# Attention followed by a squared-ReLU FFN in fp32: seven buffers for the unscaled output, loads issued ahead of stores, staged pieces of w_in

## The chip, the cores and the metric

The kernel runs on one core of a Trainium2 chip. The metric is the device time of one execution in microseconds (us). Engines are named as the profile names them: PE (TensorE, with PEld for its weight loads), DVE (VectorE), ACT (ScalarE), POOL (GpSimd) and SP (SyncE, which here only issues DMAs; SPq and ACTq are the queues of DMA issues).

## The reference

Eight batches, twelve heads, 448 tokens, 64 numbers a head. The attention's data are fp32, the two matrices of the FFN 64-bit floats; the result is fp32.

```python
q_n, k_n = rmsnorm(q, g_q), rmsnorm(k, g_k)
scores = q_n @ k_n.T / sqrt(64)
attn = exp(scores - max(scores)); attn /= sum(attn) + 1e-9
x = (attn @ v)               # as 3584 tokens x 768
h = x @ w_in                 # w_in 768 x 2048
g = s * relu(h) ** 2 + b
out = g @ w_out              # w_out 2048 x 768
```

## The kernel before

**Order of work.** The order of every engine's instructions is written out by hand: the program's order is the order on each engine and on each DMA queue. Almost all DMAs are issued by SP, one after the other; an issue that has to wait for its data or its buffer holds back all that SP issues later. Only the rows of q and k for the norms are loaded from ACT's queue (L189).

**Attention.** Two heads make a pair; there are 48 pairs, and each takes four slots of a software pipeline. `slot(i)` (L390) issues the scores, the exponentials and then the jobs that were put down for this slot (L373 to L388). For pair p these are: the load of `kqv` (L212; six buffers, so that of pair p-6 has to be free) in slot 4p-21, the spreading of the inverse norms (L219) in 4p-20, `weigh` (L294, L301: the product with v, and the sums of the exponentials on PE, in one PSUM tile `av`) in slots 4p+3 and 4p+5, and right after it `take`: ACT copies the sums to `sz` (L312, one buffer) and the unscaled output to `uz` (L313, four buffers). Later slots write the sums to DRAM and read them back across partitions (`gather` 4p+7, `fetch` 4p+9 into `zt`), invert them (DVE L324, slot 4p+12), write them and read them back spread (`put_z` 4p+13, `get_z` 4p+16), multiply on POOL (`divide` L340, 4p+18) and store x (`put_x` L343, 4p+20). Between these, 24 pieces of w_in are converted, one every seven slots (`convert` L345): the 64-bit numbers are read as two 32-bit words each and made into fp32 by DVE and ACT, and sums for the product are made by POOL. The pieces for the first four of eight column groups stay in SBUF split in two parts; the other twelve go to DRAM (`t_d`).

**The FFN's first product.** The product of 2x2 blocks is made by seven products of sums of blocks (`MUL`, L459), each in three matmuls of split operands (high x high, high x low, low x high). There are 14 runs (7 groups of 512 tokens, twice: first the column groups 0 to 3, then 4 to 7) of four blocks; n counts the 56 blocks, i the four of a run. One block, `ffn_in` (L463), is 63 matmuls of 256 columns into four PSUM banks. With eight banks, block n+1 takes those of block n-1, which `rectify` (L503) frees: ACT copies and DVE adds the seven products (L477 to L499), ACT applies the relu (L519) and SP stores r to DRAM (L520). After `ffn_in` of block n come, in this order: `rectify` of block n-1 with its store, late slots of the attention, the end of a conversion of w_out begun a block before, the begin of the next (its load, L561), and `steps(n)` (L692). `steps` prepares x for the next run, in three parts: `s_load` (SP, L441; two buffers), `s_sums` (POOL, L138 to L140), `s_split` (ACT L150, DVE L152; four buffers). In block i=0 it loads two parts, in i=1 it sums and splits the first, in i=2 it loads the third and sums the second, in i=3 it sums the third and splits the second and third. Conversions of w_out begin from n=4 on in all blocks but i=0, and from n=28 on in all. When the second half of the columns begins (n=25 to 28), `steps` also loads the twelve pieces of w_in from DRAM and splits them (`tin_load` L528, `tin_split`), through two buffers `w9`.

**The FFN's second product** (`g_load` to `store`, L579 to L657) is not touched by the change. At its end it uses the buffers `uz` of the long-lived pool for its split operand.

Of the kernel before, what the change touches and what calls it, by code (L numbers as in the profile page):

```python
# [45 lines left out]
def attention_then_relu2_ffn(  # L46
# [117 lines left out]
    def attention(ps):  # L164
# [142 lines left out]

        def take(p):
            t = avs.pop(p)
            uz = uzs[p] = lp.tile([P, 2 * TG], F32, tag="uz", bufs=4, name=f"uz{p}")  # L310
            sz = szs[p] = lp.tile([P, SEQ], F32, tag="sz", name=f"sz{p}")
            S.copy(sz, t[:, 1, :SEQ])  # L312
            S.copy(uz[:, :SEQ], t[:, 0, :SEQ])  # L313
# [133 lines left out]
    def s_sums(n):  # L447
        sums_right(s9s[n], G)

    def s_split(n):  # L450
        t = s9s.pop(n)
        to = sns[n] = pools["s"].tile([P, 2, 7, 2 * P], F32R, tag="s", bufs=NK + 1, name=f"s{n}")
        return split((to[:, 0], to[:, 1]), t[:, 1:8])

    def finish(g):
        for _ in g:
            pass
# [63 lines left out]
            r_d[q][g].rearrange("f p t -> p f t"), rt.rearrange("p (f t) -> p f t", f=2)  # L521
        )

    tls = {}

    def tin_load(q, k):
        t = tls[q, k] = pools["w9"].tile([P, 7, P], F32, tag="w9", bufs=2, name=f"tl{q}_{k}")
        nc.sync.dma_start(t.rearrange("p c f -> p (c f)"), t_d[q][k])  # L528

    def tin_split(q, k):  # L530
        to, of = t_in(q), tls.pop((q, k))
        return split((to[:, k, 0], to[:, k, 1]), of)

    touts = {}

# [128 lines left out]
    with tc.manual_schedule(engines=ORDERED):  # L664
# [4 lines left out]
        for i in range(FIRST, NSLOT + 2):  # L669
            slot(i)  # L670
            if i == NSLOT - 8:
                first.close()
                pools["s"] = pools["s9", 0] = pools["s9", 1] = pool(mid, "spool", "right")
            for n in range(NK):
                if i == NSLOT - 8 + 3 * n:
                    s_load(n)
                if i == NSLOT - 6 + 3 * n:
                    s_sums(n)
                if i == NSLOT - 5 + 3 * n:
                    finish(s_split(n))  # L680
        early.close()
        pools["w9"] = pools["t4"] = pool(ctx, "w9pool", "left")
        pools["c"] = pools["s9", 1] = pool(late, "cpool2", "left")
        ps = ctx.enter_context(
            tc.tile_pool(name="ps", bufs=1, space=PSUM, reuse_waits="tile")
        )
# [5 lines left out]
        def steps(n):  # L692

            r, g, q = blocks[n]
            i = q % QUADS
            s0 = NK * (r + 1)
            if r + 1 < len(runs):
                if i == 0:
                    s_load(s0)
                    s_load(s0 + 1)  # L700
                elif i == 1:
                    s_sums(s0)
                    finish(s_split(s0))
                elif i == 2:
                    s_load(s0 + 2)
                    s_sums(s0 + 1)
                else:
                    s_sums(s0 + 2)
                    finish(s_split(s0 + 1))
                    finish(s_split(s0 + 2))  # L710
            b = n - (NG - 1) * QUADS
            if b == 0:
                for k in range(2):
                    tin_load(QUADS, k)
            if 0 < b <= QUADS:
                u = b + QUADS - 1
                for k in range(NK):
                    finish(tin_split(u, k))
                    if k == 0:
                        tin_load(u, 2)  # L720
                    elif u + 1 < NM:
                        tin_load(u + 1, k - 1)
            if n == nb - 14:
                tout_load(0)
                tout_load(1)
            if n == nb - 13:
                finish(tout_split(0))
                finish(tout_split(1))
            b = n - (nb - QUADS)
            if b == 0:  # L730
                tout_load(2)
                tout_load(3)
            elif b > 0:
                for k in (2 * b, 2 * b + 1):
                    finish(tout_split(k))
                    tout_load(k + 2)

        for n, (r, g, q) in enumerate(blocks):
            ffn_in(r, q)
            if n:  # L740
                rectify(*blocks[n - 1])
            for i in range(3 * n, 3 * n + 3):
                if i < 20:
                    slot(NSLOT + 2 + i)
            for x in begun:
                finish(x)
            begun.clear()
            if n >= 4 and todo and (n % 4 or n >= 28):
                c = convert_out(todo.pop(0))
                next(c)  # L750
                begun.append(c)
            steps(n)
            if n == nb - QUADS - 1:
                assert not todo and not begun
                late.close()
                pools["g"] = pool(ctx, "gpool", "left")
                for x in range(3):
                    g_load(x)
            if n == nb - 3:
                g_sums(0)  # L760
                g_sums(1)
            if n == nb - 2:
                g_load(3)
                g_load(4)
# [70 lines left out]
```

## Time and profile before

| | us |
|---|---|
| median of 3 runs | 1820.38 |
| lowest and highest | 1816.62, 1824.65 |
| the profiled execution | 1828.55 |
| its span | 1826.7 |
| PE busy | 1465.4 (80%) |
| DVE, ACT, POOL busy | 1002.7, 775.2, 800.3 |

The profile is of one execution; its rows are read against that execution's own time. Busy times are sums over the span. A wait is put down to the event that came last before an instruction began. The three stages follow one another: attention to about 777 us, the first product to about 1389, the second to the end.

### The profile page before, as it was taken

What the parts mean: (1) busy time and instruction counts of PE and PEld (TensorE: products, weight loads), DVE (VectorE), ACT (ScalarE), POOL (GpSimd) and SP (SyncE); (2) the same over time, 40 slices, a digit from 0 to 9 for tenths busy, and PEclk for the clock granted to TensorE, in tenths of its full rate; (3) what the DMA queues carried; (4) which work ended last, traced back from release to release, by engine and by line L of the source; (5) the groups of instructions that cost most, each with busy time, mean ns of one, the idle gap of its engine ahead of it and who ended that gap; (6) DMA issues with size and microseconds to landing.
All of it is one profiled execution on the core that took longest, in us unless ns stands there. A gap on an engine that the chain in (4) does not pass through costs nothing. (4 is left out here: it accounts for less than half of the span.)

```text
span 1826.7 us, 26159 instructions
## 1 busy us (share of the span) xinstructions
PE 1465.4 (80%) x9760; PEld 1126.6 (62%) x9760; DVE 1002.7 (55%) x1546; ACT 775.2 (42%) x1132; POOL 800.3 (44%) x719
## 2 busy tenths in 40 slices
PE   2877777677777778898878756777887999999999
PEld 1433323233322333397877755777886899999999
DVE  3555544454444444345555555555456977767675
ACT  2555444453444444533333433333445544444443
POOL 6355544464444453333343322333321645555553
PEclk6998888898878988998989878888998999999999
DMA  7475545554656555334444444444336433333232
GB/s 212 123 192 155 152 131 147 163 164 140 170 151 183 156 157 160 88 106 156 133 139 140 146 148 150 143 135 135 135 112 217 151 94 104 100 94 104 93 109 65
DMA packets 172366, 253.71 MB, mean 139 GB/s; under 512 B 54544, under 2 KB 122832, under 8 KB 172240
## 3 DMA queue, kind: packets, MB, share of 16 engines
q1 hardware_dynamic: 165904, 231.86, 42.1%
q10 hardware_dynamic: 6336, 20.19, 3.5%
q8 instruction: 76, 1.25, 0.3%
q14 instruction: 50, 0.41, 0.1%
HBM read 183.06 MB, written 68.76 MB: 138 GB/s over the span
## 5 line engine op out<-in xcount | busy, mean ns | idle before, releaser
L471 PE MATMUL h<-s,tin 128*128 128x256 f32 x3528 | 485.2, 302 | 132.5 <-DVE r L480 57.4
L471 PEld LDWEIGHTS h<-s,tin 128*128 128x128 f32 x3528 | 469.5, 208 | 148.8 <-DVE r L480 63.9
L630 PE MATMUL m<-tout,gh 128*128 128x384 f32 x1568 | 404.1, 339 | 10.1 <-ACT gh L614 9.9
L294 PE MATMUL av<-e,kqv 128*32 128x448 f32 x1536 | 209.8, 674 | 163.8 <-ACT uz L313 162.2
L253 DVE TENSOR_REDUCE nmx<-sh 112x2 fp32r<-112x896 f32 x192 | 208.6, 1088 | 187.3 <-PE sh L244 180.9
L630 PEld LDWEIGHTS m<-tout,gh 128*128 128x128 f32 x1568 | 286.6, 190 | 11.8 <-ACT gh L614 10.8
L630 PE MATMUL m<-tout,gl 128*128 128x384 f32 x784 | 266.2, 339 | 5.9 <-DVE gl L615 5.9
L284 ACT ACTIVATE e<-st 128x896 f32<-128x896 f32 x192 | 176.4, 919 | 160.6 <-PE st L277 160.3
L294 PEld LDWEIGHTS av<-e,kqv 128*32 128x32 f32 x1536 | 45.3, 124 | 254.0 <-ACT uz L313 173.8
L594 POOL TENSOR_TENSOR g<-g 128x256 f32<-128x256 f32 x112 | 94.5, 844 | 226.6 <-DVE g L593 226.6
L273 PE MATMUL st<-kqv 64*128 64x448 f32 x768 | 182.1, 550 | 0.0
L152 DVE TENSOR_TENSOR s<-s,s 128x1792 fp32r<-128x1792 f32 x42 | 87.5, 2088 | 168.8 <-ACT s L150 165.7
L614 ACT CAST gh<-g 128x896 fp32r<-128x896 f32 x112 | 105.3, 941 | 174.0 <-POOL g L598 102.0
L615 DVE TENSOR_TENSOR gl<-g,gh 128x896 fp32r<-128x896 f32 x112 | 141.2, 1261 | 57.2 <-ACT gh L614 57.2
L480 DVE TENSOR_TENSOR r<-r,h 128x256 f32<-128x256 f32 x408 | 144.2, 415 | 39.9 <-ACT r L490 26.0
L230 POOL TENSOR_TENSOR kqv<-kqv,rb 128x448 f32<-128x448 f32 x95 | 129.8, 1376 | 66.9 <-ACT kqv L226 65.9
L340 POOL TENSOR_TENSOR uz<-uz 128x448 f32<-128x448 f32 x48 | 55.6, 1158 | 232.2 <-DMA uz<-z_d 217.3
L630 PEld LDWEIGHTS m<-tout,gl 128*128 128x128 f32 x784 | 148.4, 189 | 8.0 <-DVE gl L615 8.0
L277 PE MATMUL st<-shq,row 64*128 64x448 f32 x384 | 139.9, 720 | 3.8 <-DMA shq<-nmx 3.8
L244 PEld LDWEIGHTS sh<-kr 64*112 64x112 f32 x384 | 54.6, 278 | 140.6 <-issue 49.9
L200 DVE TENSOR_REDUCE ssq<-raw 128x14 f32<-128x896 f32 x48 | 52.1, 1085 | 159.3 <-ACT raw L195 108.5
L138 POOL TENSOR_TENSOR s<-s 128x512 f32<-128x512 f32 x42 | 55.1, 1311 | 186.3 <-DMA s<-x_d 172.1
(78 smaller groups left out, 1795.6 us busy)
## 6 DMA issues: line engine op xcount, KB each, us to landing
kqv<-in_dram SPq DMA_DIRECT2D x48, 704.0 KB
raw<-r_d SPq DMA_DIRECT2D x112, 256.0 KB
r_d<-r SPq DMA_DIRECT2D x51, 512.0 KB
rb<-i_d SPq DMA_DIRECT2D x96, 224.0 KB
raw<-in_dram ACTq DMA_DIRECT2D x44, 448.0 KB
w64i<-in_dram SPq DMA_DIRECT2D x24, 512.0 KB
w64o<-in_dram SPq DMA_DIRECT2D x32, 384.0 KB
uz<-z_d SPq DMA_DIRECT2D x96, 112.0 KB
```

Source lines behind the costliest of these rows:

```text
L230: E.tensor_tensor(of, of, rb[:, n], ALU.mult)
L253: V.tensor_reduce(out=nmxs[p][:, :, c : c + 1], in_=shs.pop(i)[:QC, :, :SEQ], op=ALU.max, axis=AX.X, negate=True,)
L273: T.matmul(st[:, j, :SEQ], t[d, 0, k0 : k0 + P], t[d, 1], start=True, stop=False)
L277: T.matmul(st[:, j, :SEQ], row[d], shq[p % 3][d], start=False, stop=True)
L284: S.activation(e, sts.pop(i)[:, :, :SEQ], AF.Exp)
L294: T.matmul(t[n * Q : (n + 1) * Q, 0, :SEQ], x[:, 2 * g + h, j, m * Q : (m + 1) * Q], e[h][:, j], start=g + h == 0, stop=g + h == 2,)
L471: T.matmul(to, w[:, lw, sa], x[:, lx, tb], start=k == n == 0 and j % 2 == 0, stop=k == NK - 1 and n == 2, skip_group_check=True,)
L480: V.tensor_tensor(to, to, part(j), op_)
L594: G.tensor_tensor(g9[:, 2:4], g9[:, 0:2], g9[:, 7:8].broadcast_to([P, 2, P]), ALU.add)
L614: S.copy(gh, g9[:, 1:8])
L615: V.tensor_tensor(gl, g9[:, 1:8], gh.bitcast(F32), ALU.subtract)
L630: T.matmul(to, g[:, sa], w, start=m == 0 and n == 0, stop=m == NM - 1 and n == 2,)
```

## The change

`take` takes three of seven `uz` tiles from the attention's own pool with three buffers, the other four as before from the long-lived pool. The four buffers of split x get a tag each, and the fourth is laid in a pool that opens when the attention's memory is given back. The loop over the blocks issues `s_load` and the begin of a conversion of w_out (its load) ahead of `rectify` with its store; conversions now begin from n=4 on in all blocks but i=2; the end of one is still worked in the block after its begin. `steps` sums two parts of x in block i=1 and the third in i=2. The pieces of w_in from DRAM go through one staging tile of six pieces: two are loaded in each of n=22, 23 and 24, and after each split the piece six further on.

```diff
         def take(p):
             t = avs.pop(p)
-            uz = uzs[p] = lp.tile([P, 2 * TG], F32, tag="uz", bufs=4, name=f"uz{p}")
+            if p % 7 < 2 or p % 7 == 6:
+                uz = ap.tile([P, 2 * SEQ], F32, tag="uz", bufs=3, name=f"uz{p}")
+            else:
+                uz = lp.tile([P, 2 * TG], F32, tag="uz", bufs=4, name=f"uz{p}")
+            uzs[p] = uz
...
     def s_split(n):
         t = s9s.pop(n)
-        to = sns[n] = pools["s"].tile([P, 2, 7, 2 * P], F32R, tag="s", bufs=NK + 1, name=f"s{n}")
+        n4 = n % (NK + 1)
+        to = sns[n] = pools["s", n4 < NK].tile([P, 2, 7, 2 * P], F32R, tag=f"s{n4}", name=f"s{n}")
...
-    def tin_load(q, k):
-        t = tls[q, k] = pools["w9"].tile([P, 7, P], F32, tag="w9", bufs=2, name=f"tl{q}_{k}")
-        nc.sync.dma_start(t.rearrange("p c f -> p (c f)"), t_d[q][k])
...
+    def tin_load(n):
+        if n >= QUADS * NK:
+            return
+        if not staged:
+            staged.append(pools["t4"].tile([P, 6, 7, P], F32, tag="t0", name="staged"))
+        q, k = divmod(n, NK)
+        nc.sync.dma_start(
+            staged[0][:, n % 6].rearrange("p c f -> p (c f)"), t_d[QUADS + q][k]
+        )
+
+    def tin_split(n):
+        q, k = divmod(n, NK)
+        to = t_in(QUADS + q)
+        return split((to[:, k, 0], to[:, k, 1]), staged[0][:, n % 6])
...
             if r + 1 < len(runs):
-                if i == 0:
-                    s_load(s0)
-                    s_load(s0 + 1)
-                elif i == 1:
+                if i == 1:
                     s_sums(s0)
+                    s_sums(s0 + 1)
                     finish(s_split(s0))
                 elif i == 2:
-                    s_load(s0 + 2)
-                    s_sums(s0 + 1)
-                else:
                     s_sums(s0 + 2)
+                elif i == 3:
                     finish(s_split(s0 + 1))
                     finish(s_split(s0 + 2))
             b = n - (NG - 1) * QUADS
-            if b == 0:
+            if -2 <= b <= 0:
                 for k in range(2):
-                    tin_load(QUADS, k)
+                    tin_load(2 * (b + 2) + k)
             if 0 < b <= QUADS:
-                u = b + QUADS - 1
                 for k in range(NK):
-                    finish(tin_split(u, k))
-                    if k == 0:
-                        tin_load(u, 2)
-                    elif u + 1 < NM:
-                        tin_load(u + 1, k - 1)
+                    finish(tin_split(NK * (b - 1) + k))
+                    tin_load(NK * (b + 1) + k)
...
         for n, (r, g, q) in enumerate(blocks):
             ffn_in(r, q)
-            if n:
-                rectify(*blocks[n - 1])
-            for i in range(3 * n, 3 * n + 3):
-                if i < 20:
-                    slot(NSLOT + 2 + i)
-            for x in begun:
-                finish(x)
-            begun.clear()
-            if n >= 4 and todo and (n % 4 or n >= 28):
+            i = q % QUADS
+            if r + 1 < len(runs):
+                if i == 0:
+                    s_load(NK * (r + 1))
+                    s_load(NK * (r + 1) + 1)
+                elif i == 2:
+                    s_load(NK * (r + 1) + 2)
+            begun_, begun[:] = begun[:], []
+            if n >= 4 and todo and i != 2:
                 c = convert_out(todo.pop(0))
                 next(c)
                 begun.append(c)
+            if n:
+                rectify(*blocks[n - 1])
+            for u in range(3 * n, 3 * n + 3):
+                if u < 20:
+                    slot(NSLOT + 2 + u)
+            for x in begun_:
+                finish(x)
             steps(n)
```

## Rows read from the trace of the kernel before

**Rows 1.** Windows by stage: length, then each engine's busy us; clock, DMA share.
```profile
102.95:716.11 613.16, 449.73 (x3054) 188.83 (x3050) 288.76 (x366) 272.66 (x375) 298.97 (x256) 0.86 0.57 158
...
776.85:1389.00 612.15, 485.02 (x3528) 469.47 (x3528) 328.40 (x629) 225.57 (x365) 206.74 (x174) 0.87 0.42 139
```

**Rows 2.** Attention, 102.95 to 716.11: a wait (us, times, longest); a group of instructions.
```profile
PE av L294 <- ACT uz L313: 159.1, 37, 6.6
...
L313 ACT COPY uz<-av 128x448 f32<-128x448 f32 x38 | 20.2, 533 | 206.0 <-DMA x_d<-uz 126.5 <-DMA rb<-i_d 49.5 <-issue 30.0
```

**Rows 3.** Timeline of a stalled pair: start, length, instruction, idle time before it.
```profile
416.00 0.35 SPq L212 DMA_DIRECT2D kqv<-in_dram  x1
...
416.46 0.56 SPq L343 DMA_DIRECT2D x_d<-uz  x1
...
423.97 0.53 ACT L313 COPY uz<-av 128x448 f32<-128x448 f32 x1 [6.32 <-DMA x_d<-uz]
...
424.56 3.22 PE L294 MATMUL av<-e,kqv 128*32 128x448 f32 x16 [5.26 <-ACT uz L313]
```

**Rows 4.** Pairs before the first stall: timeline of PE, and a window.
```profile
91.45 0.94 PE L301 MATMUL av<-e,ones 128*32 128x448 f32 x8
...
101.47 0.94 PE L301 MATMUL av<-e,ones 128*32 128x448 f32 x8
...
113.71 0.57 PE L244 MATMUL sh<-kr 64*112 64x448 f32 x2 [1.29 <-DVE nmx L253]
...
92.70:102.70 10.00, 10.00 (x82) 4.62 (x82) 7.73 (x11) 7.02 (x11) 5.35 (x4) 1.00 0.69 167
```

**Rows 5.** First product, 776.85 to 1389: waits (us, times, longest), PE's and SP's.
```profile
PE h L471 <- DVE r L480: 57.4, 15, 13.1
PE h L471 <- ACT s L150: 37.1, 16, 6.4
PE h L471 <- DVE s L152: 32.3, 21, 2.3
...
SPq L520 <- ACT r L519: 342.1, 38, 17.9
```

**Rows 6.** Timeline of PE: the first blocks of the first product.
```profile
776.85 37.01 PE L471 MATMUL h<-s,tin 128*128 128x256 f32 x294 [5.40 <-ACT uz L313]
```

**Rows 7.** Timeline of a run's first block: x load, sums, split, PE's bank.
```profile
996.78 2.57 SPq L441 DMA_DIRECT2D s<-x_d  x4
...
1004.10 1.29 POOL L138 TENSOR_TENSOR s<-s 128x512 f32<-128x512 f32 x1 [7.73 <-DMA s<-x_d]
...
1007.32 1.69 ACT L150 CAST s<-s 128x1792 fp32r<-128x1792 f32 x1 [8.97 <-POOL s L140]
...
1011.46 12.66 PE L471 MATMUL h<-s,tin 128*128 128x256 f32 x84 [6.01 <-DVE r L480]
```

**Rows 8.** Timeline of the last pair before the first stall: DVE, ACT, SP.
```profile
112.20 0.17 DVE L324 SCALAR_TENSOR_TENSOR zt<-zt 128x7 f32<-128x7 f32 x1 [3.17 <-DMA zt<-s_d]
...
114.95 0.53 ACT L312 COPY sz<-av 128x448 f32<-128x448 f32 x1 [2.01 <-DMA s_d<-sz]
...
101.71 0.33 SPq L212 DMA_DIRECT2D kqv<-in_dram  x1
...
112.96 0.39 SPq L212 DMA_DIRECT2D kqv<-in_dram  x1
```

**Rows 9.** Window of 2 us after a load of kqv; last the clock, DMA share, GB/s.
```profile
403.00:405.00 2.00, 1.27 (x10) 0.60 (x6) 1.58 (x3) 0.00 (x0) 2.00 (x3) 1.00 0.95 351
```

**Rows 10.** Timeline of DVE in a run's fourth block.
```profile
976.12 0.36 DVE L110 TENSOR_SCALAR o<-w64o 128x384 int32<-128x384 int32 x1 [4.52 <-DMA w64o<-in_dram]
```

**Rows 11.** The blocks that load pieces of w_in: a window, and timeline rows.
```profile
1042.00:1138.00 96.00, 63.38 (x443) 60.56 (x442) 51.70 (x89) 34.64 (x53) 26.55 (x24) 0.80 0.47 159
...
1075.34 0.94 ACT L150 CAST tin<-tl 128x896 fp32r<-128x896 f32 x1 [11.16 <-DMA tl<-t_d]
...
1078.61 5.16 PE L471 MATMUL h<-s,tin 128*128 128x256 f32 x21 [11.66 <-DVE r L480]
```

More of the change, by code (lines that the diff above doesn't have):

```diff
@@ L522, in rectify @@
         )
-    tls = {}
-    def tin_load(q, k):
-        t = tls[q, k] = pools["w9"].tile([P, 7, P], F32, tag="w9", bufs=2, name=f"tl{q}_{k}")
-        nc.sync.dma_start(t.rearrange("p c f -> p (c f)"), t_d[q][k])
-    def tin_split(q, k):
-        to, of = t_in(q), tls.pop((q, k))
-        return split((to[:, k, 0], to[:, k, 1]), of)
+    tls, staged = {}, []
+    def tin_load(n):
[11 more added lines that the diff above has]
+        return split((to[:, k, 0], to[:, k, 1]), staged[0][:, n % 6])
     touts = {}
@@ L672, in attention_then_relu2_ffn @@
                 first.close()
-                pools["s"] = pools["s9", 0] = pools["s9", 1] = pool(mid, "spool", "right")
+                pools["s", True] = pools["s9", 0] = pools["s9", 1] = pool(mid, "spool", "right")
             for n in range(NK):
@@ L683, in attention_then_relu2_ffn @@
         pools["c"] = pools["s9", 1] = pool(late, "cpool2", "left")
+        pools["s", False] = pool(mid, "spool2", "right")
         ps = ctx.enter_context(
```

## The prediction

> **What bounds the kernel now.** I read the windows by stage first, then the waits of TensorE (PE) in each stage, then the timelines of one stalled and one unstalled cycle. Of the span of 1826.7 us, 613 belong to 38 attention pairs and 612 to the first matrix product of the FFN [rows 1]; PE is busy 450 of the first and 485 of the second. So two stages have room; the last product, busy nearly throughout, has none.
>
> In the attention one wait explains nearly all idle time of PE: 159.1 us, 37 times, on the copy of `uz` (L313), and ScalarE itself sits idle 206.0 us ahead of 38 such copies [rows 2]. The timeline tells why [rows 3]. SP stands at the load of `kqv` until PE has used an older one; at 416.00 it goes, and only then the store of x of four pairs back (L343, 416.46). That store frees the buffer which the copy needs; the copy starts at 423.97, and PE, which waits for the bank that it empties, at 424.56 after 5.26 us of idling. So PE releases SP, SP's transfer releases ScalarE, and that PE: a ring that closes once a pair. 613.16/38 = 16.1 us a pair.
>
> What a pair costs without the ring is seen before the four buffers were used up: the last matmul groups of two pairs stand at 91.45 and 101.47, 10.02 us apart, with PE busy 10.00 of 10 us at a granted clock of 1.00 [rows 4]. In the stalled stage the mean clock is 0.86 [rows 1], so the stall also costs clock.
>
> In the FFN's first product PE waits 57.4 us for rectify's sums (banks not free), 37.1 for ScalarE's half of the split of x and 32.3 for VectorE's half [rows 5]. An undisturbed stretch gives 37.01 us for 294 matmuls, 0.126 us each [rows 6]; 3528 of them [rows 1] would be 444 us. The stage is 168 us above that: 127 of idling and 41 of slower matmuls. SP spends 342.1 us before the stores of r, waiting for the relu [rows 5], and everything queued behind waits too. In one such case the x load is issued at 996.78, lands at 1004.10, the sums on POOL are followed by the split at 1007.32, and rectify, behind that split on VectorE, frees PE's bank at 1011.46, after 6.01 us [rows 7].
>
> **The change, part by part.** *Seven buffers of uz.* The three p%7 classes in the attention's pool and the four in the long-lived one each rotate so that pair p reuses p-7's buffer. Its store is issued at slot 4p-8 and the copy stands at 4p+5, over three pairs later; before it was one slot. The wait goes; no instruction is added. The 206 us of ScalarE's idling are not the gain; PE's pace is. Late next are the small transfers behind the big ones in the same queue. They show in the one fast period that has a load of w_in [rows 8]: SP's cycle from one `kqv` to the next is 101.71 to 112.96 = 11.25 us; VectorE stood 3.17 us for `zt` until 112.20, which gave PE an idle 1.29 at 113.71 [rows 4]; `sz`, of which there is one buffer, held ScalarE 2.01 us until 114.95. About every second pair loads w_in (24 pieces in 48 pairs). Half of 10.02 and half of 11.25 is 10.6. No store of x ran yet in those periods: 224 KB (128 x 448 x 4 bytes) at the 351 GB/s of a busy stretch [rows 9] is 0.65 us a pair, if it adds at all. I take 0.4: **11.0 us a pair**. Bounds: 10.02 if all is hidden, and 13.5, midway to today's 16.1 less a little, if the queue's latencies come round to PE. Gain 38 x (16.1 - 11.0) = 194 us, say 195; ends 99 and 231. The DMA engines leave room for it: a share of 0.57 of 16.1 us [rows 1] is 9.2 us of full occupancy a pair, so they would stand at 84%. That is close, and is why I don't take 10.02.
>
> The Trainium skill (DMA: Bandwidth & Descriptors, section Specifications) gives about 358 GB/s of HBM bandwidth to a core. At 158 GB/s for 16.1 us a pair moves 2.5 MB, an estimated 7.1 us by that page against the 9.2 that the row gives; by the page DMA would be far from the bound and the pair 10.02 us, a gain of 231.
>
> *x loads and the loads of w_out ahead of the store of r.* On SP they no longer stand behind the wait for the relu; they still wait for their buffer, which the split of the run before frees, and then the store waits behind them. The relu of the block before comes late in the block anyway, so I put that delay at nothing; if the split is late the store is late with it, and the r buffer is reused only four blocks later (about 32 us of cover). The x load of a run starts up to a block (8 us) sooner, which covers the 6.01 us case [rows 7]. *Sums a block sooner*: POOL does two of a run's three in its second block; the splits stay where they were, so they find the sums done. Cost: POOL's instructions are the same in number. *Begin of a conversion not in the run's third block*: no conversion is worked in its fourth block, where two splits stand. Now VectorE stands there 4.52 us for w_out [rows 10], with the split behind it, and that goes. With 3 pieces in 4 blocks from the fifth on, 32 pieces last until about block 47 instead of 42, still before their first use in the last runs; no cost.
>
> Per run of four blocks (32 us of PE work): outside 1042 to 1138 the stage is 516 us for 3085 matmuls (388 us): 128 us over some 12 runs, 10.7 a run. What stays: in every second run a conversion's POOL sums stand before the sums of x, so a split comes 2 to 5 us late, and a little clock. I leave 5 a run: 12 x 5.7 = 68 us gained, ends 15 and 110.
>
> *Six staged pieces of w_in.* From 1042 to 1138 PE is busy 63.38 of 96 us, at a clock of 0.80, with 443 matmuls, or 56 us at full pace [rows 11]: 40 us lost. With two buffers each piece is loaded only when the one before is split: ScalarE waited 11.16 us for a piece, the copies for rectify stood behind it, and PE idled 11.66 [rows 11]. Six pieces, loaded two blocks ahead, take that out; I leave an ordinary run's loss, 12 us: 28 gained, ends 10 and 36. The staging tile lies where `rfirst` lay, whose last store is some 17 blocks old: no wait.
>
> Renaming the split's four buffers and giving one a pool of its own: nothing, same rotation. First pairs, last pairs, last product: unchanged.
>
> **Sum.** Gains 195 + 68 + 28 = 291 us. The profiled execution took 1828.55 (span 1826.7): 1537.5. The median of the runs, 1820.38, is 8 lower, so **1530 us**.
>
> **Rivals.**
> *The queue takes the ring's place* (0.17). The loop by way of x's store goes, but `zt` and `sz` of a pair lie behind 2.5 MB, and their latency stretches each pair to 13.5 us. For it: the 3.17 and 2.01 us [rows 8]. Against: both came with only 1.29 us of PE idling [rows 4]. Time: 1828.5 - 99 - 96 - 8 = 1625.
> *The FFN stage keeps its pace* (0.15). VectorE and ScalarE work in order, and a late split only changes place; the gain is 15 + 10. For it: 342.1 us of SP's waits become waits for a split instead. Against: VectorE is busy 328 of 612 us [rows 1]. Time: 1828.5 - 195 - 25 - 8 = 1600.
> *All is hidden* (0.12): 10.02 us a pair, ends of the FFN parts: 1828.5 - 231 - 146 - 8 = 1443; between that and the forecast lie most such cases, about 1480.
> *VectorE and POOL exclude each other* (0.03). If their work could not overlap, a pair would cost the sum of both, (288.76 + 298.97)/38 = 15.5 us [rows 1], a gain of only 23: 1828.5 - 23 - 96 - 8 = 1701. Against: in a fast 10 us VectorE shows 7.73 and POOL 5.35 [rows 4], 13.1 in all, so they do overlap. The Trainium skill (SBUF — State Buffer, section SBUF: two separate sides) states this lock, for GpSimd against VectorE's forms with two SBUF inputs or two ports; by that row it binds for few of them.
> *Slower* (0.02): at a run's first block SP stands at the x load for its buffer, the store of r, the next loads and in the end rectify's buffer stand behind it, and PE waits twice a run as long as its worst wait today, 13.1 us [rows 5]. The FFN gains vanish, 13 x 26.2 = 341 is added: 1828.5 - 195 + 341 - 8 = 1966. It decides from 15 us a run on (195/13). Against: that buffer is freed within the same block.
> *The change does not do what it says* (0.02): another wait of the same length, of the same store, stays: 1820. The rotation speaks against it.
> The forecast itself: 0.49.
>
> **Numbers.** 1470 to 1640 holds the forecast with its bounds (pairs of 10.2 to 12 us), the queue, the FFN rival and most of the hidden case; left out are the best ends, the lock, slower and no effect. A measurement of this kernel can tell 0.5% from no change. Faster 0.96, same 0.02, slower 0.02.
>
> **What would show it.** Right: no wait of L313 for the store of x; pairs 10.5 to 12 us apart; clock in the attention above 0.95; DMA share there above 0.75; the FFN's first product at 500 to 535 us; no wait of ScalarE for `tl`. Step by step wrong: a pair above 12.5 us, with PE behind `sz`, `zt` or shq; PE in the FFN stage still waiting over 80 us; SP waits at the x load longer than those before the store today. The forecast as a whole falls if the attention is not over 130 us shorter.

## The result and the profile after

The changed kernel takes 1565.98 us (median of 4 runs, 1563.83 to 1570.89); the kernel before took 1822.52 on the same chip. The ratio is 0.859, with a 95% interval of 0.854 to 0.864. The profiled execution took 1566.36 us (span 1564.6), 262.2 less than that of before.

Windows of the changed kernel, as in [rows 1]: stretch and its length, busy us (and instructions) of PE, PEld, DVE, ACT and POOL, granted clock, DMA share, GB/s. The first is 38 attention pairs, from the fourth copy of `uz` to the 42nd; the second is the FFN's first product; the third lies inside it, the blocks that split pieces of w_in from DRAM.

```profile
104.42:543.11 438.69, 393.21 (x3038) 183.36 (x3034) 272.97 (x363) 272.89 (x376) 316.01 (x256) 0.97 0.79 219
...
604.80:1126.90 522.10, 457.66 (x3528) 446.29 (x3528) 339.89 (x630) 223.66 (x366) 199.19 (x176) 0.94 0.49 164
...
826.07:898.40 72.33, 56.66 (x418) 54.35 (x418) 53.47 (x85) 32.39 (x51) 28.38 (x21) 0.91 0.59 204
```

The pairs go from 613.16 to 438.69 us [rows 1], 174.5 less; 438.69/38 = 11.54 us a pair. The clock rose from 0.86 to 0.97 and the DMA share from 0.57 to 0.79. The first product goes from 612.15 to 522.10 us, 90 less. From its end to the end of the span is 437.7 us in both kernels. So the two stages hold the whole difference.

In the attention, groups by line in the first of these windows: instructions, then busy us, mean ns, idle time before them and what ended it. `uz` is L317 here, `sz` L316, `zt` L328.

```profile
L317 ACT COPY uz<-av 128x448 f32<-128x448 f32 x39 | 21.0, 538 | 0.0
...
L316 ACT COPY sz<-av 128x448 f32<-128x448 f32 x39 | 20.6, 528 | 46.4 <-DMA s_d<-sz 39.8 <-PE sh L244 4.2 <-PE av L301 2.2
...
L328 DVE SCALAR_TENSOR_TENSOR zt<-zt 128x7 f32<-128x7 f32 x38 | 8.2, 216 | 83.5 <-DMA zt<-s_d 75.8 <-DMA i_d<-ri 7.8
...
L294 PE MATMUL av<-e,kqv 128*32 128x448 f32 x1216 | 130.8, 548 | 5.2 <-ACT uz L317 5.2
L244 PE MATMUL sh<-kr 64*112 64x448 f32 x302 | 73.3, 473 | 39.0 <-DVE nmx L253 32.1 <-ACT uz L317 5.0 <-ACT sz L316 1.7
```

ScalarE's 206.0 us ahead of the copy of `uz` and PE's 159.1 us behind it [rows 2] have become 0.0 and 5.2. In their place stand the small transfers: ScalarE waits 39.8 us until the sums have left `sz`, and VectorE 75.8 us until they come back in `zt`; PE feels both only in part. PE is busy 10.35 us a pair and idle 1.20. Two cases, as a timeline (start, length, idle time before):

```profile
311.02 0.53 ACT L316 COPY sz<-av 128x448 f32<-128x448 f32 x1 [4.06 <-DMA s_d<-sz]
...
312.04 1.71 PE L294 MATMUL av<-e,kqv 128*32 128x448 f32 x16 [1.40 <-ACT uz L317]
...
330.91 0.17 DVE L328 SCALAR_TENSOR_TENSOR zt<-zt 128x7 f32<-128x7 f32 x1 [4.17 <-DMA zt<-s_d]
...
331.23 1.04 DVE L253 TENSOR_REDUCE nmx<-sh 112x2 fp32r<-112x896 f32 x1
...
331.76 0.54 ACT L317 COPY uz<-av 128x448 f32<-128x448 f32 x1
...
332.41 0.73 PE L244 MATMUL sh<-kr 64*112 64x448 f32 x2 [2.29 <-ACT uz L317]
```

In the first, PE stands 1.40 us behind ScalarE, which stood 4.06 at `sz`. In the second, VectorE's reduction behind `zt` ends at 332.27 and ScalarE's copy of `uz` at 332.30, so PE's 2.29 us belong to both and not to the copy alone.

In the first product, the waits (us in total, times, longest) that answer to [rows 5]; L476 is the matmul, L485 VectorE's adds of `rectify`, L525 the store of r and L445 the load of x:

```profile
PE h L476 <- DVE r L485: 39.2, 20, 8.2
PE h L476 <- DVE s L152: 17.5, 12, 1.6
PE h L476 <- ACT s L150: 6.9, 7, 1.6
...
SPq L525 <- ACT r L524: 162.5, 48, 7.0
SPq L445 <- DVE r L485: 91.0, 20, 9.3
SPq L445 <- DVE s L152: 35.8, 14, 3.2
```

PE's three waits fall from 126.8 to 63.6 us. SP still waits, but now at the load of x for its buffer (126.8 us) and half as long at the store (162.5 for 342.1 [rows 5]).

### The profile page after: what moved, and what is told of

Same layout as the page of the kernel before. It is cut to its first block, busy times and chain, and to the rows that moved or that the text cites. A ratio compares the mean times of both kernels' runs of the same rounds, so it can differ in the third digit from the quotient of the medians.

```text
span 1564.6 us, 26152 instructions
## 1 busy us (share of the span) xinstructions
PE 1385.4 (89%) x9760; PEld 1101.2 (70%) x9760; DVE 1000.1 (64%) x1546; ACT 773.4 (49%) x1132; POOL 807.5 (52%) x719
## 4 chain that ended last, share of the span: by engine, by line
PE 47%; DMA 16%; DVE 12%; issue 11%; ACT 6%; POOL 5%; SPq 2%; ACTq 0%; POOLq 0%; DVEq 0%
PE m L642 24%; PE st L273 6%; PE av L294 6%; PE h L476 4%; DMA zt<-s_d 3%; DVE r L485 3%; DMA raw<-in_dram 3%; PE sh L244 3%; PE av L301 2%; ACT s L150 2%; DVE nmx L253 2%; DVE s L152 2%; PE st L277 2%; DMA s<-x_d 2%; DMA i_d<-ri 2%
## 5 line engine op out<-in xcount | busy, mean ns | idle before, releaser
L476 PE MATMUL h<-s,tin 128*128 128x256 f32 x3528 | 457.9, 293 | 68.6 <-DVE r L485 39.2
L476 PEld LDWEIGHTS h<-s,tin 128*128 128x128 f32 x3528 | 446.3, 198 | 80.8 <-DVE r L485 46.3
L606 POOL TENSOR_TENSOR g<-g 128x256 f32<-128x256 f32 x112 | 94.4, 843 | 230.7 <-DVE g L605 230.7
L273 PE MATMUL st<-kqv 64*128 64x448 f32 x768 | 188.2, 563 | 0.0
L294 PE MATMUL av<-e,kqv 128*32 128x448 f32 x1536 | 165.1, 547 | 7.5 <-ACT uz L317 5.2
L485 DVE TENSOR_TENSOR r<-r,h 128x256 f32<-128x256 f32 x408 | 144.0, 415 | 37.0 <-ACT r L495 26.3
L244 PE MATMUL sh<-kr 64*112 64x448 f32 x384 | 94.2, 481 | 80.1 <-DVE nmx L253 41.7
L277 PE MATMUL st<-shq,row 64*128 64x448 f32 x384 | 145.7, 742 | 3.8 <-DMA shq<-nmx 3.8
L344 POOL TENSOR_TENSOR uz<-uz 128x448 f32<-128x448 f32 x48 | 65.1, 1357 | 149.3 <-DMA uz<-z_d 149.3
L203 POOL TENSOR_TENSOR ri<-ri,mhalf 128x14 f32<-128x14 f32 x48 | 137.2, 2859 | 4.0
L138 POOL TENSOR_TENSOR o<-o 128x384 f32<-128x384 f32 x16 | 16.2, 1011 | 238.1 <-DVE o L119 184.3
L610 POOL TENSOR_TENSOR g<-g 128x256 f32<-128x256 f32 x112 | 133.5, 1192 | 0.0
```

What stands on the lines that cost most here:

```text
L203: G.tensor_tensor(ri, ri, mhalf[:, :n], ALU.pow)
L244: T.matmul(sh[:QC, j, :SEQ], t[d, 1].rearrange("k (p c) -> k c p", c=NQ)[:, c], t[d, 0], start=True, stop=True,)
L273: T.matmul(st[:, j, :SEQ], t[d, 0, k0 : k0 + P], t[d, 1], start=True, stop=False)
L277: T.matmul(st[:, j, :SEQ], row[d], shq[p % 3][d], start=False, stop=True)
L294: T.matmul(t[n * Q : (n + 1) * Q, 0, :SEQ], x[:, 2 * g + h, j, m * Q : (m + 1) * Q], e[h][:, j], start=g + h == 0, stop=g + h == 2,)
L476: T.matmul(to, w[:, lw, sa], x[:, lx, tb], start=k == n == 0 and j % 2 == 0, stop=k == NK - 1 and n == 2, skip_group_check=True,)
```

## The experiments

**Each part alone, or taken back.** First the seven buffers alone, on the kernel before (with the split's buffers renamed, as in the change):

```diff
-            uz = uzs[p] = lp.tile([P, 2 * TG], F32, tag="uz", bufs=4, name=f"uz{p}")
+            if p % 7 < 2 or p % 7 == 6:
+                uz = ap.tile([P, 2 * SEQ], F32, tag="uz", bufs=3, name=f"uz{p}")
+            else:
+                uz = lp.tile([P, 2 * TG], F32, tag="uz", bufs=4, name=f"uz{p}")
+            uzs[p] = uz
...
```

> The kernel before with the seven buffers of uz alone (and the split's buffers laid as in the change, to make room). Theory (the attention's gain is this part's alone, and the stages add): the attention ends near 605 us as in the changed kernel, the FFN's first product stays at about 612 us, 1650 us in all. Rival (the earlier x loads or other parts of the change also help the attention): the attention ends after 640 us and the time is above 1685.

Measured: 1653.21 us, ratio 0.908 (0.905 to 0.912). Its windows of the pairs and of the first product:

```profile
103.18:539.05 435.87, 395.25 (x3040) 183.83 (x3038) 272.65 (x363) 272.89 (x375) 309.04 (x256) 0.97 0.79 220
...
600.10:1212.70 612.60, 478.06 (x3527) 463.20 (x3528) 328.13 (x629) 225.90 (x365) 209.81 (x176) 0.87 0.42 139
```

The buffers are worth 1820.81 - 1653.21 = 167.6 us by themselves. Pairs and attention clock are those of the changed kernel, and the first product is as long as before, at its old clock.

The reverse, the changed kernel with four buffers:

```diff
-            if p % 7 < 2 or p % 7 == 6:
-                uz = ap.tile([P, 2 * SEQ], F32, tag="uz", bufs=3, name=f"uz{p}")
-            else:
-                uz = lp.tile([P, 2 * TG], F32, tag="uz", bufs=4, name=f"uz{p}")
-            uzs[p] = uz
+            uz = uzs[p] = lp.tile([P, 2 * TG], F32, tag="uz", bufs=4, name=f"uz{p}")
```

> The changed kernel with four buffers of uz as before. Theory: the attention is back at about 777 us, the FFN's first product stays at about 522 us, about 1738 us in all. Rival (part of the FFN's gain comes from a faster attention, by its late slots that run beside the first blocks): the first product is longer than 540 us and the time above 1756.

Measured: 1729.31 us, ratio 0.949 (0.946 to 0.953), pairs of 15.8 us. The ring's wait is back, as a row of the attention's waits shows (the copy is L313 here):

```profile
PE av L294 <- ACT uz L313: 146.3, 38, 6.2
```

1729.31 - 1565.98 = 163.3 us for the same buffers, against 167.6 alone: the part does nothing to the FFN, and the FFN's parts nothing to it.

The changed kernel without the staging tile, pieces of w_in loaded and split through two buffers as before:

```diff
-        q, k = divmod(n, NK)
-        nc.sync.dma_start(
-            staged[0][:, n % 6].rearrange("p c f -> p (c f)"), t_d[QUADS + q][k]
-        )
+    def tin_load(q, k):
+        t = tls[q, k] = pools["w9"].tile([P, 7, P], F32, tag="w9", bufs=2, name=f"tl{q}_{k}")
+        nc.sync.dma_start(t.rearrange("p c f -> p (c f)"), t_d[q][k])
...
```

> The changed kernel with the pieces of w_in loaded through two buffers as before. Theory (the staging is worth the 28 us of the prediction): about 1594 us, with ScalarE waiting for tl again and PE standing over 10 us twice. Rival (with the loads ahead of the store the two buffers would have done): within 10 us of 1566.

Measured: 1580.44 us, ratio 0.868 (0.865 to 0.870): 14.5 over the changed kernel, between the two. The first product itself takes 538.6 us against 522.1. A row of its waits there:

```profile
ACT tin L150 <- DMA tl<-t_d: 23.3, 4, 8.1
```

The wait that staging is there to remove is real, and the changed kernel has none such; but it costs little more than half of what I had put on it.

Staging and buffers with the old order of loads, sums and conversions (the loads and sums of x, left out of the cut, go back to their places in the kernel before, too):

```diff
...
-            if n >= 4 and todo and i != 2:
-                c = convert_out(todo.pop(0))
-                next(c)
-                begun.append(c)
...
-            for x in begun_:
+            for x in begun:
                 finish(x)
+            begun.clear()
+            if n >= 4 and todo and (n % 4 or n >= 28):
+                c = convert_out(todo.pop(0))
+                next(c)
+                begun.append(c)
```

> The changed kernel with the order of loads, sums and conversions of before; seven buffers and staging stay. Theory (the order is worth what is left of the first product's gain, 90 - 28 us): about 1628 us, PE waiting again for ScalarE's and VectorE's splits. Rival (the staging carries most of the stage's gain): below 1600 us.

Measured: 1638.46 us, ratio 0.899 (0.895 to 0.902); the first product takes 592.6 us against 522.1, and the order is worth 1638.46 - 1565.98 = 72.5 us. The window of the first product of this kernel, and PE's waits in it:

```profile
606.80:1199.40 592.60, 480.75 (x3528) 464.74 (x3528) 331.54 (x629) 225.54 (x365) 213.22 (x176) 0.89 0.44 144
...
PE h L476 <- ACT s L150: 43.7, 16, 6.2
PE h L476 <- DVE r L485: 36.5, 16, 5.9
PE h L476 <- DVE s L152: 31.5, 25, 2.3
```

Against the changed kernel, what the order takes away is PE's wait for the split of x (43.7 + 31.5 us here, 6.9 + 17.5 there), not the one for rectify's sums. The stage is 592.60 - 522.10 = 70.5 us longer than in the changed kernel: 47 of that are PE's idling (111.9 against 64.4), and 23 are slower matmuls, at a granted clock of 0.89 against 0.94. Loads, sums and conversions were moved back together, so which of the three carries the gain is not shown. From the seven buffers alone to this kernel is 1653.21 - 1638.46 = 14.8 us, staging's share once more.

**What holds a pair at 11.5 us.** A measure first: the kernels above that keep the seven buffers, and the one with the sums first below, have the changed kernel's attention, and their profiled executions show 11.40 to 11.56 us a pair. A difference of less than 0.2 us a pair is therefore not told from none. The inversion of the sums and what follows it, one or two slots later, so that `zt` has longer to land:

```diff
-            at(s0 + 12, invert, p)
-            at(s0 + 13, put_z, p)
-            at(s0 + 16, get_z, p)
-            at(s0 + 18, divide, p)
-            at(s0 + 20, put_x, p)
+            at(s0 + 14, invert, p)
+            at(s0 + 15, put_z, p)
+            at(s0 + 17, get_z, p)
+            at(s0 + 19, divide, p)
+            at(s0 + 21, put_x, p)
```

> The changed kernel with the inversion of the sums two slots later (slots 14 and 15 instead of 12 and 13), its reading back and the division and store of x one slot later. Theory (a pair takes 11.8 us instead of 10.0 because VectorE, in order, stands for zt, 75.8 us in all, and PE's scores behind it): the waits for zt fall below 20 us, the pairs to about 11.2 us, 1566 - 25 = about 1541 us. Rival (the transfers of a pair themselves are the bound, the wait for zt only shows it): another wait takes its place, the pairs stay at 11.6 us or more, 1558 us or more.

Measured: 1573.17 us, ratio 0.862 (0.858 to 0.866); pairs 11.49, against 11.54. The waits for `zt` went as the theory said, the pairs did not follow. Two rows of its waits, 104 to 560 us:

```profile
ACT sz L316 <- DMA s_d<-sz: 81.8, 30, 6.5
...
PE av L294 <- ACT uz L317: 43.4, 25, 4.6
```

VectorE no longer waits for `zt` to land, but ScalarE stands twice as long at `sz` (39.8 before), with the copy of `uz` behind it and PE behind that. The total also carries something else: the late slots of the attention now reach further into the first blocks of the FFN, where PE waits 5.6 us for rectify's sums in `rfirst` (0.6 in the changed kernel).

The small transfers of the sums issued by ScalarE, not behind SP's big loads:

```diff
-            nc.sync.dma_start(s_d[p], szs.pop(p)[0:P:Q])
+            nc.scalar.dma_start(s_d[p], szs.pop(p)[0:P:Q])
...
-            nc.sync.dma_start(zt, s_d[p].rearrange("(h j) (p c) -> (j p) h c", h=2, c=TILES))
+            nc.scalar.dma_start(zt, s_d[p].rearrange("(h j) (p c) -> (j p) h c", h=2, c=TILES))
```

> The changed kernel with the two small transfers of the sums (sz to DRAM, DRAM to zt) issued from ScalarE's queue instead of SP's. Theory (they are late because they are issued and carried behind the big transfers of SP's queue): the waits for zt and sz together fall from 116 us to under 50, the pairs to 11.2 us or less, about 1540 us. Rival (all queues share the same engines, so they land as late from any queue): waits and pairs as before, within 10 us of 1566; or slower, where ScalarE now waits to issue.

Measured: 1562.34 us, ratio 0.855 (0.850 to 0.859); pairs 11.45. Rows of its waits, 104 to 560 us:

```profile
PE av L294 <- ACT uz L317: 36.5, 26, 3.1
ACT kqv L226 <- DMA i_d<-ri: 25.9, 11, 4.7
...
DVE zt L328 <- DMA zt<-s_d: 4.4, 5, 2.0
```

The wait for `zt` goes from 75.8 to 4.4 us, and the pair is as long as it was: ScalarE is now late, and stands at the scaling of `kqv` too. The Trainium skill (DMA: Bandwidth & Descriptors, section Issuing engines are not separate DMA queues) says that transfers of all issuing engines run on the same 16 DMA engines, and that another issuer saves only the time of issuing, usually small beside the transfer. The total agrees, and so do the timelines: the sums leave sooner, and no row shows them travelling faster. The write of `sz` is issued 3.6 us (median of the pairs) after ScalarE's copy, against 7.3 when it stood in SP's order. In the five cases where VectorE still waited for `zt`, it began 7.2 us after the issue of the reading back, against 5.4 in the 31 cases of the changed kernel. Only that the saving is small does not hold here: 3.7 us of standing before the issue are much beside 5.4 us to landing.

Two buffers for `sz`:

```diff
-            sz = szs[p] = lp.tile([P, SEQ], F32, tag="sz", name=f"sz{p}")
+            sz = szs[p] = (lp if p % 2 else ap).tile([P, SEQ], F32, tag="sz", name=f"sz{p}")
```

> The changed kernel with two buffers of sz. Theory (sz holds ScalarE 39.8 us, but PE stands only some 13 us behind it): the wait for s_d goes, 5 to 15 us gained, 1551 to 1561 us. Rival (the ring by way of sz is the new bound of the attention): the pairs fall below 11 us, 1535 us or less.

Measured: 1557.60 us, ratio 0.854 (0.850 to 0.859); pairs 11.23. The wait for `sz` is gone; PE's largest one in the attention stays:

```profile
PE sh L244 <- DVE nmx L253: 36.3, 20, 4.5
```

That is the loop by way of VectorE, which still stands 66.8 us at `zt`. The gain of 8 us is inside what was expected, though the two intervals overlap; that the pairs are 0.31 shorter, below all of 11.40 to 11.56, is the clearer sign.

**The waits left in the FFN.** POOL's sums of x ahead of its sums for w_out:

```diff
-                    s_sums(s0)
-                    s_sums(s0 + 1)
                     finish(s_split(s0))
-                elif i == 2:
-                    s_sums(s0 + 2)
...
+            if r + 1 < len(runs):
+                if i == 1:
+                    s_sums(NK * (r + 1))
+                    s_sums(NK * (r + 1) + 1)
+                elif i == 2:
+                    s_sums(NK * (r + 1) + 2)
             for x in begun_:
                 finish(x)
```

> The changed kernel with POOL's sums of x issued ahead of the sums of the conversion of w_out in the same block. Theory (what is left of PE's waits for rectify, 39.2 us, comes from splits that wait for POOL, which first sums w_out): those waits fall below 20 us and the first product to about 500 us, about 1545 us. Rival (the splits and the sums of rectify themselves fill VectorE; the order on POOL changes only who waits): 1560 us or more.

Measured: 1554.55 us, ratio 0.852 (0.848 to 0.856); the first product takes 514.3 us, 7.8 less. Waits there:

```profile
PE h L476 <- DVE r L485: 17.8, 19, 3.0
PE h L476 <- DVE s L152: 18.1, 12, 1.6
PE h L476 <- ACT s L150: 14.0, 11, 1.7
```

PE's wait for rectify's sums falls from 39.2 to 17.8 us and its longest from 8.2 to 3.0, but the wait for the split of x grows by 7. About half of what was expected, and not all of that is the edit's: of the 11.3 us between the profiled executions, 5.7 lie in the attention's pairs, which it does not touch. The stage's 514.3 us lie below the 520 to 529 that it takes in the other kernels with the changed kernel's FFN and its inversion, so this part is clear.

**All of these together** (the edits of the later inversion, the two `sz` and the sums first, none new):

> The changed kernel with three edits at once: the inversion later (as in the run that moved it), two buffers of sz, and POOL's sums of x first. Theory A (the waits for zt and for sz are two loops of nearly the same length, so taking one alone only bares the other): with both gone the pairs fall to 10.6 us or less, the attention ends before 570 us, and with 11 us of the FFN the time is about 1520 us. Theory B (the data of a pair, carried by one queue at a DMA share of 0.79, are the bound, and these waits only show it): the pairs stay at 11.2 us or more, SP's own waits grow, and the time is about 1545 us, the two gains of 9 and 11 us measured singly.

Measured: 1545.12 us, ratio 0.847 (0.844 to 0.851). That interval lies below the changed kernel's: it beats both kernels, by 20.9 us the changed one. The window of its pairs, 11.07 us each:

```profile
106.66:527.18 420.52, 392.91 (x3046) 176.41 (x3042) 305.02 (x364) 273.03 (x375) 313.33 (x253) 0.98 0.83 226
```

Between the profiled executions 24.6 us are gained (1566.36 to 1541.73): 18.2 in the pairs (438.69 - 420.52) and 5.4 in the first product (522.10 to 516.74). The time is the one of Theory B, in which the single gains simply add: 8.4 for the two `sz`, 11.4 for the sums first, none for the later inversion. Its pairs of 11.2 or more are not met, nor are Theory A's 10.6 or less. On the pairs the two `sz` alone gave 12.0 us and the later inversion alone 1.9; the 4.3 by which both together exceed that lie inside the 6.3 by which kernels with the same attention differ (433.0 to 439.4). So it is not shown that one wait only bares the other. What stays, 0.73 us of PE's idling a pair, has no single wait in front.

Five buffers of `uz`, one from the attention's pool:

```diff
-            if p % 7 < 2 or p % 7 == 6:
-                uz = ap.tile([P, 2 * SEQ], F32, tag="uz", bufs=3, name=f"uz{p}")
+            if p % 5 == 3:
+                uz = ap.tile([P, 2 * SEQ], F32, tag="uz", bufs=1, name=f"uz{p}")
```

> The changed kernel with five buffers of uz instead of seven. Theory (one pair more is enough, since the store of five pairs back is issued over a pair, some 14 us, ahead of the copy and lands in about 7): within 8 us of 1566, no wait of L313's copy for the store of x. Rival (with the transfers now dense, the store lands more than a pair late, and it takes seven): ScalarE waits for the store again, 1580 us or more.

Measured: 1561.72 us, ratio 0.855 (0.853 to 0.857); pairs 11.49, and no wait for the store of x. One buffer more than before is enough.

**The bytes.** Fewer of them, with the same instructions on PE:

```diff
+            if p > 4 and p % 2:
+                raws[p] = raws[p - 1]
+                return
...
-            w = ep.tile([P, 2, 2 * P, 2], I32, tag="w64", bufs=2, name=f"w64i{n}")
+            if n % 2 == 0:
+                w64s[0] = ep.tile([P, 2, 2 * P, 2], I32, tag="w64", bufs=2, name=f"w64i{n}")
+            w = w64s[0]
...
```

> The changed kernel with every second load of the rows of q and k (from pair 5 on) and every second load of w_in in the attention left out; the work on them is done on the tile loaded before, so only bytes are missing (about 350 of 2500 KB a pair). Theory B (bytes are the bound): the pairs fall in proportion, from 11.5 us towards PE's 10.0, to 10.4 us or less, about 1522 us. Theory A (the length of the loops through small transfers, not the bytes, is the bound): 11.1 us or more, 1550 us or more.

Measured: 1540.85 us, ratio 0.844 (0.842 to 0.846). The window of its pairs, 10.80 us each:

```profile
103.31:513.88 410.57, 387.16 (x3042) 180.66 (x3040) 271.53 (x363) 272.93 (x375) 304.11 (x256) 0.99 0.73 199
```

199 GB/s for 10.80 us is 2.15 MB a pair, against 219 for 11.54 or 2.53 MB: 15% less to move makes a pair 6% shorter. Neither theory is right alone. The transfers count, but a pair is not simply as long as they take. How the bytes act, the timelines tell in part: where VectorE waited for `zt`, it began 5.2 us (median) after SP's issue, and 5.2 to 5.6 in the kernels with the changed kernel's attention, so the sums do not land clearly sooner. But SP issues the write of `sz` 6.0 us after ScalarE's copy, and in those kernels 7.1 to 7.4. Why SP comes to it sooner was not traced.

Both, the fewer bytes with the later inversion and the two `sz`:

> The changed kernel with the later inversion, two buffers of sz and the missing bytes of the run before (half of the rows of q and k and of w_in in the attention not loaded, the work done on the tile before); POOL's order in the FFN as in the changed kernel. Each alone left the pairs at 11.07 and 10.80 us, against 11.54 in the changed kernel and 10.02 undisturbed. Theory (bytes and the loops through small transfers act on the same thing, the time at which a small transfer lands behind the big ones, and together they take the rest): 10.4 us or less, PE's waits in these pairs under 12 us in all, about 1524 us. Rival (what is left is something else, as matmuls at a lower pace or SP's issue time): 10.7 us or more, 1535 us or more.

Measured: 1532.80 us, ratio 0.836 (0.831 to 0.842); pairs 10.51. Window and waits of its pairs:

```profile
102.60:502.16 399.56, 387.36 (x3048) 175.97 (x3046) 300.14 (x364) 274.18 (x375) 319.39 (x253) 1.00 0.78 203
```

```profile
PE av L297 <- ACT uz L320: 6.4, 6, 2.0
PE sh L247 <- DVE nmx L256: 4.2, 8, 1.5
...
PE sh L247 <- ACT kr L238: 1.3, 1, 1.3
```

PE is idle 12.2 us of 399.6, 0.32 a pair, at a clock of 1.00. Its busy time is 10.19 a pair; a little above the 10.02 of [rows 4], which held no store of x. So the waits for small transfers and the bytes together account for 1.03 of the 1.52 us that a pair had above 10.02. The result lies between the theory (10.4 us or less, 1524) and the rival (10.7 or more, 1535). Its time holds a longer first product, too: 534.1 us against 522.1, at a clock of 0.92 against 0.94.

## Why the prediction was right, and where it was off

The forecast was 1530, the median is 1565.98: inside the range, faster, by the mechanism named, and 36 us above. On the profiled executions the gain is 262.2 of 291, 29 short: 20.5 in the pairs, 6 in the first product, the rest outside both. The other 7 are the 8 us taken off because the median lay below the profiled execution; in the changed kernel the two are alike (1565.98 and 1566.36).

- **Seven buffers, 195 forecast, 174.5 measured** on the pairs; 163 to 168 in the time of whole kernels. The ring was the bound: taken out alone it gives its whole gain, put back it takes it. "Late next are the small transfers behind the big ones in the same queue" held: `zt` and `sz` lead the waits. What was mis-sized is the pair, **11.0 us, which measured 11.54**: 38 x 0.54 = 20.5 us. The 10.6 came from one unstalled pair with a load of w_in and one without, and the 0.4 for x's store from its bytes. In the steady stage PE idles 1.20 us a pair and is busy 10.35, not 10.02, at a clock of 0.97 where [rows 4] had 1.00. That this is the wait for `zt` alone fell with the later inversion (11.49); that it is `sz` alone, with the two buffers (11.23); both took the pair to 11.07, fewer bytes alone to 10.80, all three to 10.51. So the waits at `sz` and the bytes each have a part; whether the two waits are loops of about equal length that hide each other is not shown, and how much of it x's store has was not tried.
- **The clock** went from 0.86 to 0.97 in the stage from which the stall was taken, and stayed at 0.87 in the other one as long as that kept its waits (seven buffers alone).
- **Order, 68 forecast, about 72 measured** (70.5 in the stage itself). The mechanism is the one given, as far as the waits show it: the split of x found its sums in time. That the size came out so well says nothing of its three parts, which were not priced or tried singly. A third of it is clock, which the forecast did not price apart. What was left, rectify behind a split that waits for POOL, was named as "a conversion's POOL sums stand before the sums of x"; putting them behind took 7.8 us of the stage. The store of r, now behind the load of x, cost nothing visible: the forecast for SP was waits below 342 us, and they are 126.8.
- **Staging, 28 forecast, 14.5 and 14.8 measured** (16.5 and 20.0 in the stage itself). The step that failed is "I leave an ordinary run's loss, 12 us". In the window 826.07 to 898.40 the 418 matmuls at 0.126 us [rows 6] are 52.7 us of 72.33: some 20 us are still lost. The loads are in time, but three splits of w_in still stand in VectorE's and ScalarE's order ahead of rectify, as the timeline shows:

```profile
846.05 1.69 ACT L150 CAST s<-s 128x1792 fp32r<-128x1792 f32 x1 [6.46 <-POOL s L140]
847.64 2.61 ACT L150 CAST tin<-staged 128x896 fp32r<-128x896 f32 x3
847.76 2.04 DVE L152 TENSOR_TENSOR s<-s,s 128x1792 fp32r<-128x1792 f32 x1 [7.59 <-ACT s L150]
849.73 4.16 DVE L152 TENSOR_TENSOR tin<-staged,tin 128x896 fp32r<-128x896 f32 x3
...
854.28 4.00 PE L476 MATMUL h<-s,tin 128*128 128x256 f32 x16 [8.24 <-DVE r L485]
```

  Here the split of x comes late (POOL), and with it the three of w_in, 4.16 us on VectorE, and then PE by 8.24. This is the longest of PE's waits in the stage.
- **Nothing for the rest.** First pairs, the transition and the last product are as they were, as forecast.

The signs: no wait for the store of x (right), pairs of 10.5 to 12 us (11.54), clock above 0.95 (0.97), DMA share above 0.75 (0.79), first product of 500 to 535 us (522.1), no wait for a staged piece (right), PE's waits there below 80 us (522.10 - 457.66 = 64.4 of idling in all).

Of the rivals, **the queue in the ring's place** is half true: fewer bytes and shorter waits for its small transfers do shorten the pair, but it stands at 11.54 and not at 13.5 us. **The FFN keeps its pace** fell with the old order (592.6 against 522.1 us). **All hidden** asked for 10.02; even with fewer bytes and few small waits it is 10.51. **The exclusion of VectorE and POOL** would have held a pair at 15.5; it exists between some instructions, as the last section shows. The reading against it is weaker than it looked: the profile books standing for the other engine as busy time, so 13.1 us of busy time in 10 us [rows 4] do not show by themselves that the work overlapped. **Slower** asked for SP standing at the load of x; its longest wait there is 9.3 us, and PE's longest fell from 13.1 to 8.2.

## What to carry to other kernels

When a ring of buffers is the bound, count how many slots lie between a buffer's last read and its next write: here a single buffer more gave all that three more did. Price what comes after it not from the first undisturbed cycle, but from one that carries all the traffic of the steady state; here the two differ by half a microsecond a cycle. The length of a wait in the list is not what its removal gains: 75.8 us of VectorE's gave nothing, twice, 39.8 us of ScalarE's took 12 us off the pairs. Before two waits are called coupled, compare what both give together with the sum of the single gains, and that difference with how far equal kernels lie apart.

## What was not expected

- Taking 70 us of waits off one engine moved the total by less than can be told, twice (the later inversion, ScalarE as issuer), while two buffers of `sz` made a pair 0.31 us shorter, and 0.47 with the later inversion.
- The DMA engines were not at their limit at a share of 0.79: with the small waits out they ran at 0.83 and 226 GB/s over 420 us, with shorter pairs. Even so 15% fewer bytes made pairs 0.74 us shorter. So the bytes did not act as a ceiling; what was seen is that SP issued the sums sooner, not that these landed sooner after their issue.
- POOL and VectorE do exclude each other, between some instructions. In the kernel with the later inversion the instruction on `zt` (L328, 128x7, two operands) takes 820 ns on average, against 216 in the changed kernel. Its group and, from the timelines, one case:

```profile
L328 DVE SCALAR_TENSOR_TENSOR zt<-zt 128x7 f32<-128x7 f32 x39 | 32.0, 820 | 0.5 <-DMA zt<-s_d 0.3
```

```profile
320.43 1.14 DVE L328 SCALAR_TENSOR_TENSOR zt<-zt 128x7 f32<-128x7 f32 x1
...
320.05 1.49 POOL L344 TENSOR_TENSOR uz<-uz 128x448 f32<-128x448 f32 x1
```

  VectorE's instruction begins while POOL multiplies and ends 0.03 us behind it, at 321.57 and 321.54. So do all 31 that took over 0.4 us: each ends within 0.04 us of the end of a POOL instruction of 128x448, 128x256 or 128x128 that had begun before it. The edit only made it frequent: in the kernel before, 16 of the 38 took over 0.5 us, each to the end of POOL's multiplication on `kqv` (L230). The Trainium skill (SBUF — State Buffer, section SBUF: two separate sides) states this: of a GpSimd instruction that reads SBUF and a VectorE one with two SBUF inputs, the first to start holds the shared port until its end. These rows agree, for the seven-element instruction above all. Others do not: in the changed kernel 17 of the 35 short ones begin and end inside POOL's power of 128x14 (L203), and that lasts its usual 2.6 us. The case at 330.91 above is one:

```profile
329.94 2.60 POOL L203 TENSOR_TENSOR ri<-ri,mhalf 128x14 f32<-128x14 f32 x1
```

  The profile has no wait for this on either engine; it shows in durations alone. POOL's multiplication on `kqv` takes 1.1 us in most cases of the changed kernel, and 1.8 to 2.5 where a two-operand instruction of VectorE of 0.68 us (L112, L114, L119) lies inside it. In the kernel with all the edits together the mean of the instruction on `zt` is 961 ns, 38 x 0.75 = 28 us of VectorE more than in the changed one; whether the pairs would be shorter without that was not tried.
